# Forgetting attention followed by a tanh-shrink MLP: first-half rows first in the MLP, and q and k of batches 3 to 7 turned a slot sooner

## The chip, the core and the metric

The kernel runs on one core of a Trainium2 chip. A core has five engines with queues of their own: TensorE (PE in the profile; PEld is its weight loads), VectorE (DVE), ScalarE (ACT), GpSimd (POOL) and SyncE (SP). DMA transfers are issued by SP and POOL here. Each engine works through its queue strictly in the order in which it was written, and engines wait for one another and for transfers through semaphores. The metric is the device time of one execution in microseconds (us), lower is better; a kernel's time is the median of its runs.

## The reference

```python
scores = q @ k.T / sqrt(64)                      # 8 batches, 8 heads, 576 tokens, head size 64
cum    = cumsum(log(clip(f, 1e-4, 1)))           # per head, along the tokens
scores = where(causal, scores + cum[i] - cum[j], -1e9)
attn   = softmax(scores)                         # over j
x      = (attn @ v) as [8*576 tokens, 8*64]      # 4608 x 512
h      = x @ w_in                                # 512 -> 2048
out    = (h - tanh(h)) @ w_out                   # 2048 -> 512
```

## The kernel before

Attention runs over 32 pairs of heads, four pairs for each batch. The emission loop (lines 423 to 440) goes through 33 *slots* `p`. Slot `p` emits the seven score tiles of pair `p` (`scores`, numbered `ti` 0 to 6, each some matmuls, one exponential on ACT and a mask on POOL), after tile 2 the `values` products of the pair before, whose result DVE normalises into `xn` (lines 294 to 296), and after tile 3 the `turn` of that pair, two DMA transposes on SP that put `xn` into the ring `XR` with features on partitions (lines 310 and 312). `b` is a batch, and `p0 = 4(b-1)` is the first slot of the batch before it; the scores of batch `b` begin in slot `p0 + 4`.

The dictionary `LOADS` (lines 192 to 225) names further work by slot and tile: it is emitted right after the scores of that tile. For batches 3 to 7 this is

- `load_block`: one of five token blocks of q or k from HBM (POOL issues it, line 94);
- `turn_block`: a DMA transpose on SP (line 99) of one block into `TQ` or `TK`, single buffers with two heads on the 128 partitions;
- `place`: a DVE copy (line 102) of 64 partitions x 1152 elements from `TQ` or `TK` into `QT` or `KT`, the operands of the scores. It reads all tokens, so it needs all five transposes. A batch has four places for q and four for k.

Batches 0 to 2 come in another way (`trans`: TensorE transposes in the slot before, evicted by ACT for `QT`, line 242, and by DVE for `KT`, line 244).

The MLP works on nine *units* of 512 tokens. A unit is a list of 30 steps: 16 `mlp1` steps (four matmuls of 512 columns over the 512 features, then tanh on ACT, line 327, then DVE adds into `gq`, line 331), and 14 `mlp2` steps (eight matmuls of 256 columns each, line 352). `mlp2` is a Strassen-Winograd product: the 512 x 2048 input is cut into blocks A11, A12 (first 256 tokens; first and second half of the 2048 rows of `h`), A21, A22 (last 256 tokens), and seven products of the list `STEPS` (two steps each) replace eight. Their left sides S1 = A21 + A22, S2 = S1 - A11, S3 = A11 - A21 (written over A21) are DVE operations at line 337, in two groups of four row blocks each; S4 = A12 - S2 (over A12) is line 374. In step `s` of `mlp1` the half is `s % 2`: rows of both halves take turns, so every block is complete only after step 15. Results leave PSUM through ACT (`m1`, line 368) or DVE (line 358: outputs `ost` and running sums `u2`, `u3`), and go out by DMA from SP (line 364).

The steps are mixed into the slots: 15 in every two slots, so four slots hold the 30 steps of one unit, and the pattern repeats with each batch. One pool of four PSUM buffers (`ps_m`) serves `mlp1`, `mlp2` and the transposes of `trans`; `values` has one buffer. PE, DVE, POOL and SP run in exactly the order of emission; ACT's order is the scheduler's.

Of the kernel before, what the change touches and what calls it, by code (L numbers as in the profile page):

```python
# [8 lines left out]
FP32 = mybir.dt.float32  # L9
FP16 = mybir.dt.float16  # L10
AF = mybir.ActivationFunctionType
ALU = mybir.AluOpType
# [9 lines left out]
def kernel(  # L22
# [10 lines left out]
    nc = tc.nc  # L33
    P = 128
# [13 lines left out]
    HU = 256  # L48
    HE = DM // 2
    NCH = DM // P  # L50
    UW = 512
# [9 lines left out]
    acc = ctx.enter_context(tc.tile_pool(name="acc", bufs=1))  # L61
# [7 lines left out]
    W1 = wpl.tile([P, NK, HE], FP16)  # L69
    W2 = wpl.tile([P, NK, HE], FP16)  # L70
    W4 = wpl.tile([P, NK, HE], FP16)
    B11, B12 = wout[:, 0:NK, 0:HE], wout[:, 0:NK, HE:DM]
    B21, B22 = wout[:, NK:NFT, 0:HE], wout[:, NK:NFT, HE:DM]
# [6 lines left out]
    qb, kb = ([t[:, 0:NJ * DM].rearrange("p (n e) -> p n e", n=NJ) for t in raw] for raw in (qraw, kraw))  # L80
    vn = [qkp.tile([P, NJ, H, VW], FP16, tag=f"vn{i}", name=f"vn{i}") for i in range(2)]
    QT = [qkp.tile([D + 3, H, S], FP16, tag=f"QT{i}", name=f"QT{i}") for i in range(2)]
    KT = [qkp.tile([D + 3, H, PITCH], FP16, tag=f"KT{i}", name=f"KT{i}") for i in range(2)]
    TQ = qkp.tile([P, NPAIR, S], FP16, tag="TQ", name="TQ")
    TK = qkp.tile([P, NPAIR, S], FP16, tag="TK", name="TK")

    def load_qk(dst, src, b, h0, h1):
        nc.gpsimd.dma_start(
            out=dst[b % 2][:, h0:h1, :, :].rearrange("p h n d -> p h (n d)"),
            in_=src[b, h0:h1, :, :].rearrange("h (p n) d -> p h (n d)", n=NT6))  # L90

    def load_block(dst, src, b, n):
        pn = min(P, S - n * P)
        nc.gpsimd.dma_start(out=dst[b % 2][0:pn, n, :].rearrange("p (h d) -> p h d", h=H),  # L94
                            in_=src[b, :, n * P:n * P + pn, :].rearrange("h p d -> p h d"))

    def turn_block(dst, src, b, n):
        pn = min(P, S - n * P)
        nc.sync.dma_start_transpose(out=dst[:, :, n * P:n * P + pn], in_=src[b % 2][0:pn, n, :])

    def place(dst, src, b, a, c):
        nc.vector.tensor_copy(out=dst[b % 2][0:D, 2 * c + a:2 * c + 3 + a:2, 0:S], in_=src[a * D:(a + 1) * D, c:c + 2, :])  # L102
# [81 lines left out]
    def load_win(f0, f1):  # L184
        nc.gpsimd.dma_start(out=win[:, :, f0:f1],
                            in_=moe_w_in[:, f0:f1].rearrange("(c p) f -> p c f", p=P))

    def load_wout(t0, t1):
# [3 lines left out]
    LOADS = {(0, 1): [lambda: load_qk(qn, q, 1, 0, 2), lambda: load_qk(kn, k, 1, 0, 2)],  # L192
             (0, 4): [lambda: load_qk(qn, q, 1, 2, H)],
             (1, 0): [lambda: load_qk(kn, k, 1, 2, H)],
             (1, 2): [lambda: load_win(0, DFF // 2)],
             (1, 5): [lambda: load_v_rest(1), lambda: load_v_head(1, 0)],
             (2, 1): [lambda: load_v_head(1, 1), lambda: load_win(DFF // 2, DFF)],
             (4, 0): [lambda: load_wout(0, NFT // 2)],
             (4, 2): [lambda: load_wout(NFT // 2, NFT)]}
    for n in range(NJ - 1):  # L200
        LOADS.setdefault((3, n), []).append(lambda n=n: load_v_block(1, n, 2, H))
    for n in range(2):
        ks = slice(n * NK // 2, (n + 1) * NK // 2)
        for i, (o, x, y) in enumerate(((W1, B12, B11), (B12, B22, B12), (W2, B22, W1), (W4, B21, W2))):
            LOADS.setdefault((NPAIR + 1 + i // 2, (3, 5, 1, 4)[i] + n), []).append(lambda o=o, x=x, y=y, ks=ks: nc.vector.tensor_tensor(
                out=o[:, ks, :], in0=x[:, ks, :], in1=y[:, ks, :], op=ALU.subtract))
    LOADS.setdefault((NPAIR, 5), []).append(lambda: load_qk(qn, q, 2, 0, H))
    LOADS.setdefault((NPAIR, 6), []).append(lambda: load_qk(kn, k, 2, 0, H))
    for b in range(2, B):
        p0 = (b - 1) * NPAIR  # L210
        for n in range(NJ - 1):
            LOADS.setdefault((p0 + 1, n), []).append(lambda b=b, n=n: load_v_block(b, n, 0, H))
        LOADS.setdefault((p0 + 1, 4), []).append(lambda b=b: load_v_rest(b))
        LOADS.setdefault((p0, 0), []).append(lambda b=b: load_aug(b))
        if b < FAR:
            continue
        for n in range(NJ):
            LOADS.setdefault((p0 - 1, n), []).append(lambda b=b, n=n: load_block(qb, q, b, n))
            LOADS.setdefault((p0, n), []).append(lambda b=b, n=n: load_block(kb, k, b, n))
            LOADS.setdefault((p0, 4), []).append(lambda b=b, n=n: turn_block(TQ, qb, b, n))  # L220
            LOADS.setdefault((p0 + 1, 4), []).append(lambda b=b, n=n: turn_block(TK, kb, b, n))
        for n, (dst, src) in enumerate(((QT, TQ), (KT, TK))):
            for a in range(2):
                for c in (0, 2):
                    LOADS.setdefault((p0 + 3, 2 * n + a), []).append(lambda b=b, dst=dst, src=src, a=a, c=c: place(dst, src, b, a, c))

    E, XN, GQ, SQ, M2 = {}, {}, {}, {}, {}

# [83 lines left out]
        nc.sync.dma_start_transpose(out=XR[:, c, r0 + S - D:r0 + S], in_=xn[D:P, NJ - 1, :])  # L312

    def mlp1(u, s):
        pr, half = divmod(s, 2)
        ft = half * NK + pr
        hps = ps_m.tile([P, UW], FP32, tag="m", name="hps")
        t0 = u * UW % RING
        parts = [(0, t0, min(UW, RING - t0))]
        if t0 + UW > RING:  # L320
            parts.append((RING - t0, 0, t0 + UW - RING))
        for o, t, n in parts:
            for ci in range(NCH):
                nc.tensor.matmul(out=hps[:, o:o + n], lhsT=win[:, ci, ft * P:(ft + 1) * P],  # L324
                                 rhs=XR[:, ci, t:t + n], start=(ci == 0), stop=(ci == NCH - 1))
        th = tmp.tile([P, UW], FP32, tag="th", name="th")
        nc.scalar.activation(out=th, in_=hps, func=AF.Tanh, scale=-1.0)  # L327
        if s % 8 == 0:
            GQ[(u, s // 8)] = gtp.tile([P, 2, NK // 2, UW], FP16, tag="gq", name="gq")
        gq = GQ[(u, s // 8)]  # L330
        nc.vector.tensor_tensor(out=gq[:, half, pr % 4, :], in0=hps, in1=th, op=ALU.add)  # L331
        if s % 8 == 7:
            sq = SQ[(u, s // 8)] = gtp.tile([P, 2, NK // 2, HU], FP16, tag="sq", name="sq")
            a11, a21, a22 = gq[:, 0, :, 0:HU], gq[:, 0, :, HU:UW], gq[:, 1, :, HU:UW]
            for o, x, y, op in ((sq[:, 0], a21, a22, ALU.add), (sq[:, 1], sq[:, 0], a11, ALU.subtract),
                                (a21, a11, a21, ALU.subtract)):
                nc.vector.tensor_tensor(out=o, in0=x, in1=y, op=op)  # L337

    LHS = {"A11": lambda u, i: GQ[(u, i)][:, 0, :, 0:HU], "A12": lambda u, i: GQ[(u, i)][:, 1, :, 0:HU],
           "A22": lambda u, i: GQ[(u, i)][:, 1, :, HU:UW], "S3": lambda u, i: GQ[(u, i)][:, 0, :, HU:UW],  # L340
           "S1": lambda u, i: SQ[(u, i)][:, 0], "S2": lambda u, i: SQ[(u, i)][:, 1]}
    LHS["S4"] = LHS["A12"]
    STEPS = [("A11", B11), ("A12", B21), ("S2", W2), ("S3", B12), ("S1", W1), ("A22", W4), ("S4", B22)]

    def mlp2(u, s):
        n, m = divmod(s, 2)
        lhs, rhs = STEPS[n]
        if m == 0:
            M2["ps"] = ps_m.tile([P, 2, HE], FP32, tag="m", name="ops")
        ps = M2["ps"]  # L350
        for kt in range(NK):
            nc.tensor.matmul(out=ps[:, m, :], lhsT=LHS[lhs](u, kt // 4)[:, kt % 4, m * P:(m + 1) * P],  # L352
                             rhs=rhs[:, kt, :], start=(kt == 0), stop=(kt == NK - 1))
        if m == 0:
            return

        def plus(src, to):
            nc.vector.tensor_tensor(out=to, in0=ps, in1=src, op=ALU.add)  # L358
            return to

        def total(src, r, e):
            ost = plus(src, tmp.tile([P, 2, HE], FP32, tag="ost", name="ost", bufs=3))
            r0 = u * UW + r * HU
            nc.sync.dma_start(out=out[r0:r0 + HU, e * HE:(e + 1) * HE].rearrange("(m p) e -> p m e", p=P), in_=ost)

        if lhs == "A11":
            M2["m1"] = acc.tile([P, 2, HE], FP32, tag="m1", name="m1")
            nc.scalar.activation(out=M2["m1"], in_=ps, func=AF.Copy)
        elif lhs == "S2":
            M2["u2"] = plus(M2["m1"], acc.tile([P, 2, HE], FP32, tag="u2", name="u2"))  # L370
        elif lhs == "A12":
            total(M2["m1"], 0, 0)
            for i in range(2):
                nc.vector.tensor_tensor(out=LHS["S4"](u, i), in0=LHS["A12"](u, i), in1=LHS["S2"](u, i), op=ALU.subtract)
        elif lhs == "S3":
            M2["u3"] = plus(M2["u2"], acc.tile([P, 2, HE], FP32, tag="u3", name="u3"))
        elif lhs == "S1":
            total(M2["u3"], 1, 1)
            plus(M2["u2"], M2["u2"])
        elif lhs == "A22":  # L380
            total(M2["u3"], 1, 0)
        else:
            total(M2["u2"], 0, 1)
# [3 lines left out]
    def att_items(p):  # L387
# [29 lines left out]
        return items  # L417

    mlp = [(fn, u, s) for u in range(NU) for fn, n in ((mlp1, NFT), (mlp2, 2 * len(STEPS))) for s in range(n)]
    TAKE = (0, 0, 0, 0, 2, 7, 6, 6, 6)  # L420
    at = 0
    with tc.manual_schedule(engines={PE, mybir.EngineType.Pool, mybir.EngineType.SP, mybir.EngineType.DVE}):
        for p in range(len(pairs) + 1):
            b, c = divmod(p, NPAIR)
# [7 lines left out]
            given, n = 0, 0  # L432
# [38 lines left out]
```

## Time and profile before

| | |
|---|---|
| median of three runs | 369.44 us (369.12 to 370.68) |
| profiled execution | 373.72 us, span of its instructions 371.6 us |
| TensorE clock granted | 0.983 of full |
| busy of the span | PE 91%, DVE 76%, PEld 63%, ACT 58%, POOL 44% |
| DVE adds into `gq` (line 331) | 144 x 688 ns |
| DVE places (line 102) | 20 x 612 ns for `QT`, 20 x 583 ns for `KT` |
| DVE Strassen sums (line 337) | 54, 692 to 743 ns |

Busy PE time is modelled and counts matmuls that queue behind one another; idle time of an engine matters only where another engine waits for it. The profiled execution is one run with its own time, so sums made from its rows are read against 373.72 us and then carried to the median.

### The profile page before, as it was taken

The page shows a single profiled execution, that of the slowest core. Times are in us where ns is not written, and L with a number is a line of the kernel's source. Part 1 is how long each engine was busy: PE and PEld are TensorE (multiplying, and loading weights), DVE is VectorE, ACT ScalarE, POOL GpSimd, SP SyncE. Part 2 cuts the span into 40 slices and gives each one's busy share as a digit, 9 for nine tenths or more (in the row PEclk, how much of TensorE's full clock was granted, in tenths as well). Part 3 has the DMA queues.
Part 4 walks back from the last instruction along what each step waited for, and adds up shares of the span by engine and source line. Part 5 has one row for each costly group of instructions (what it writes and reads, how often), then busy time and mean ns, then how long its engine had stood idle before and what let it go on. Part 6 is the DMA issues. An engine that isn't in the chain of part 4 may idle for free.

```text
span 371.6 us, 8348 instructions
## 1 busy us (share of the span) xinstructions
PE 337.5 (91%) x3156; PEld 232.4 (63%) x3156; DVE 280.7 (76%) x477; ACT 215.6 (58%) x402; POOL 164.8 (44%) x340
## 2 busy tenths in 40 slices
PE   1798986999888999899989998999999999999995
PEld 0466543786447855685568886855685577477474
DVE  7575489876689569956995689668957885885873
ACT  6568886567854487448744774477547731531520
POOL 7977552586245744584457535752222220000000
PEclk9999899899989999999999999999999999999998
DMA  9999999699957997899499979996032013002002
GB/s 105 155 182 189 181 199 81 47 122 161 160 44 56 166 185 83 67 157 184 84 79 158 141 124 83 151 181 91 16 96 54 16 46 102 0 30 85 2 29 85
DMA packets 145323, 38.78 MB, mean 104 GB/s; under 512 B 128084, under 2 KB 144196, under 8 KB 145284
## 3 DMA queue, kind: packets, MB, share of 16 engines
q0 software_dynamic: 92416, 18.37, 66.2%
q1 hardware_dynamic: 52868, 19.90, 26.7%
q8 instruction: 24, 0.39, 0.5%
q14 instruction: 15, 0.12, 0.1%
HBM read 36.85 MB, written 9.44 MB: 125 GB/s over the span
## 4 chain that ended last, share of the span: by engine, by line
PE 55%; DVE 25%; ACT 9%; issue 6%; DMA 3%; POOL 1%; POOLq 0%; DVEq 0%; SPq 0%; ACTq 0%
PE ops L352 26%; PE hps L324 13%; PE ps L266 9%; DVE gq L331 8%; ACT e L272 4%; PE av L290 4%; ACT th L327 4%; DVE QT L102 3%; DVE sq L337 3%; DVE xn L296 3%; DVE KT L244 2%; PE t L235 2%; DMA XR<-xn 2%; DVE KT L102 1%; DVE gq L337 1%
## 5 line engine op out<-in xcount | busy, mean ns | idle before, releaser
L324 PE MATMUL hps<-XR,win 128*128 128x512 f16 (+1 forms) x640 | 144.0, 362 | 5.1 <-DVE gq L331 3.9
L272 ACT ACTIVATE e<-ps 128x512 f16<-128x512 f32 x192 | 111.7, 601 | 43.7 <-PE ps L266 41.9
L327 ACT ACTIVATE th<-hps 128x512 f32<-128x512 f32 x144 | 87.0, 606 | 66.1 <-PE hps L324 54.4
L331 DVE TENSOR_TENSOR gq<-hps,th 128x512 f16<-128x512 f32 x144 | 97.7, 688 | 34.2 <-ACT th L327 32.7
L280 POOL TENSOR_SCALAR_AFFINE_SELECT e<-e 128x128 f16<-128x128 f16 (+1 forms) x192 | 67.0, 352 | 100.8 <-ACT e L272 98.9
L324 PEld LDWEIGHTS <-win 128*128 128x128 f16 x640 | 58.6, 98 | 55.9 <-issue 10.2
L266 PE MATMUL ps<-QT,KT 67*128 67x64 f16 (+4 forms) x384 | 80.0, 295 | 11.5 <-DMA KT<-clo 4.6
L352 PEld LDWEIGHTS <-gq 128*128 128x128 f16 x720 | 67.6, 98 | 21.8 <-DVE gq L331 10.2
L352 PE MATMUL ops<-wout,gq 128*128 128x256 f16 x576 | 74.6, 275 | 7.2 <-DVE gq L331 7.0
L266 PEld LDWEIGHTS <-KT 67*128 67x128 f16 x384 | 37.8, 103 | 37.3 <-issue 14.3
L358 DVE TENSOR_TENSOR ost<-ops,u 128x512 f32<-128x512 f32 x27 | 18.7, 691 | 28.1 <-PE ops L352 28.0
L290 PEld LDWEIGHTS <-e 128*128 128x128 f16 x896 | 34.3, 100 | 4.7 <-POOL e L280 1.0
L352 PE MATMUL ops<-W,sq 128*128 128x256 f16 x288 | 36.4, 272 | 0.0
L290 PE MATMUL av<-vn,e 128*128 128x65 f16 x896 | 35.3, 197 | 0.9 <-POOL e L280 0.9
L352 PEld LDWEIGHTS <-sq 128*128 128x128 f16 x288 | 27.1, 97 | 4.8
L113 POOL DMA_DIRECT2D vn<-in_v_dram x32 | 27.9, 874 | 2.3 <-issue 2.3
L296 DVE TENSOR_TENSOR xn<-av,rs 128x640 f16<-128x640 f32 x32 | 26.4, 824 | 1.1
L94 POOL DMA_DIRECT2D qn<-in_q_dram x25 | 21.2, 846 | 2.6 <-issue 2.6
L94 POOL DMA_DIRECT2D kn<-in_k_dram x25 | 21.1, 845 | 1.8 <-issue 1.7
L280 POOL TENSOR_SCALAR_AFFINE_SELECT el<-el 128x128 f16<-128x128 f16 x32 | 9.7, 303 | 26.8 <-ACT el L272 26.5
L244 DVE COPY KT<-t 64x576 f16<-64x576 f16 x24 | 19.1, 797 | 0.3
L352 PE MATMUL ops<-W,gq 128*128 128x256 f16 x144 | 18.2, 272 | 0.0
(58 smaller groups left out, 230.6 us busy)
## 6 DMA issues: line engine op xcount, KB each, us to landing
out_dram<-ost SPq DMA_DIRECT2D x36, 256.0 KB
vn<-in_v_dram POOLq DMA_DIRECT2D x24, 128.0 KB, 5.6
qn<-in_q_dram POOLq DMA_DIRECT2D x20, 128.0 KB, 3.8
kn<-in_k_dram POOLq DMA_DIRECT2D x20, 128.0 KB, 4.6
win<-in_moe_w_in_dram POOLq DMA_DIRECT2D x2, 1024.0 KB, 11.8
wout<-in_moe_w_out_dram POOLq DMA_DIRECT2D x2, 1024.0 KB, 11.0
XR<-xn SPq DMA_TRANSPOSE x56
vn<-in_v_dram POOLq DMA_DIRECT2D x12, 64.0 KB, 5.0
```

The source lines that it names most:

```text
L94: nc.gpsimd.dma_start(out=dst[b % 2][0:pn, n, :].rearrange("p (h d) -> p h d", h=H), in_=src[b, :, n * P:n * P + pn, :].rearrange("h p d - ...
L113: nc.gpsimd.dma_start(out=vn[b % 2][:, n, h0:h1, 0:D], in_=v[b, h0:h1, n * P:(n + 1) * P, :].rearrange("h p d -> p h d"))
L244: nc.vector.tensor_copy(out=to, in_=of)
L266: nc.tensor.matmul(out=ps[:, col:col + n], lhsT=KT[b % 2][:, h, j * P:(j + 1) * P], rhs=QT[b % 2][:, h, i0:i0 + n])
L272: nc.scalar.activation(out=e[:, lo:hi], in_=ps[:, lo:hi], func=AF.Exp, scale=qscale)
L280: nc.gpsimd.affine_select(out=view, in_=view, compare_op=ALU.is_ge, fill=0.0, base=0, pattern=pat, channel_multiplier=-1)
L290: nc.tensor.matmul(out=av[:, a, ib, :], lhsT=E.pop((b, c, a, j, ib)), rhs=vn[b % 2][:, j, 2 * c + a, 0:D + 1], start=(j == 0), stop=(j == ib))
L296: nc.vector.tensor_tensor(out=xn.rearrange("p i (a d) -> p a i d", a=2), in0=av[:, :, :, 0:D], in1=rs.to_broadcast([P, 2, NJ, D]), op=ALU. ...
L324: nc.tensor.matmul(out=hps[:, o:o + n], lhsT=win[:, ci, ft * P:(ft + 1) * P], rhs=XR[:, ci, t:t + n], start=(ci == 0), stop=(ci == NCH - 1))
L327: nc.scalar.activation(out=th, in_=hps, func=AF.Tanh, scale=-1.0)
L331: nc.vector.tensor_tensor(out=gq[:, half, pr % 4, :], in0=hps, in1=th, op=ALU.add)
L352: nc.tensor.matmul(out=ps[:, m, :], lhsT=LHS[lhs](u, kt // 4)[:, kt % 4, m * P:(m + 1) * P], rhs=rhs[:, kt, :], start=(kt == 0), stop=(kt ...
```

## The change

Three things are edited.

1. `mlp1` takes four steps of the first half, then four of the second, and again. A11 and A21 are complete after step 11 rather than 15. S3 is made as soon as a group's first half is there (`s % 8 == 3`); at `s % 8 == 7` S2 is made from A22 and S3, and S1 from S2 and A11.
2. `STEPS` puts S3 second: A11, S3, A12, S2, S1, A22, S4. The result of the S3 product is now copied out of PSUM by ACT (a second copy of 128 x 512 elements in each unit), and `u3` is the DVE sum of two SBUF tiles.
3. For batches 3 to 7 the loads and transposes of q and k are emitted one slot sooner. The eight places, which all stood in slot `p0 + 3`, are spread: four for `QT` in slot `p0` after tiles 0, 2, 4 and 6, two for `KT` in slot `p0 + 2` and two in slot `p0 + 3`, after tiles 1 and 5.

```diff
-            LOADS.setdefault((p0 - 1, n), []).append(lambda b=b, n=n: load_block(qb, q, b, n))
-            LOADS.setdefault((p0, n), []).append(lambda b=b, n=n: load_block(kb, k, b, n))
-            LOADS.setdefault((p0, 4), []).append(lambda b=b, n=n: turn_block(TQ, qb, b, n))
-            LOADS.setdefault((p0 + 1, 4), []).append(lambda b=b, n=n: turn_block(TK, kb, b, n))
-        for n, (dst, src) in enumerate(((QT, TQ), (KT, TK))):
-            for a in range(2):
-                for c in (0, 2):
-                    LOADS.setdefault((p0 + 3, 2 * n + a), []).append(lambda b=b, dst=dst, src=src, a=a, c=c: place(dst, src, b, a, c))
+            LOADS.setdefault((p0 - 2, n), []).append(lambda b=b, n=n: load_block(qb, q, b, n))
+            LOADS.setdefault((p0 - 1, n), []).append(lambda b=b, n=n: load_block(kb, k, b, n))
+            LOADS.setdefault((p0 - 1, 4), []).append(lambda b=b, n=n: turn_block(TQ, qb, b, n))
+            LOADS.setdefault((p0, 4), []).append(lambda b=b, n=n: turn_block(TK, kb, b, n))
+        spots = ((p0, 0), (p0, 2), (p0, 4), (p0, 6), (p0 + 2, 1), (p0 + 2, 5), (p0 + 3, 1), (p0 + 3, 5))
+        parts = [(dst, src, a, c) for dst, src in ((QT, TQ), (KT, TK)) for a in range(2) for c in (0, 2)]
+        for spot, (dst, src, a, c) in zip(spots, parts):
+            LOADS.setdefault(spot, []).append(lambda b=b, dst=dst, src=src, a=a, c=c: place(dst, src, b, a, c))
...
-        pr, half = divmod(s, 2)
+        half, pr = s % 8 // 4, s // 8 * 4 + s % 4
...
+        a11, a21, a22 = gq[:, 0, :, 0:HU], gq[:, 0, :, HU:UW], gq[:, 1, :, HU:UW]
+        if s % 8 == 3:
+            nc.vector.tensor_tensor(out=a21, in0=a11, in1=a21, op=ALU.subtract)
         if s % 8 == 7:
             sq = SQ[(u, s // 8)] = gtp.tile([P, 2, NK // 2, HU], FP16, tag="sq", name="sq")
-            a11, a21, a22 = gq[:, 0, :, 0:HU], gq[:, 0, :, HU:UW], gq[:, 1, :, HU:UW]
-            for o, x, y, op in ((sq[:, 0], a21, a22, ALU.add), (sq[:, 1], sq[:, 0], a11, ALU.subtract),
-                                (a21, a11, a21, ALU.subtract)):
-                nc.vector.tensor_tensor(out=o, in0=x, in1=y, op=op)
+            nc.vector.tensor_tensor(out=sq[:, 1], in0=a22, in1=a21, op=ALU.subtract)
+            nc.vector.tensor_tensor(out=sq[:, 0], in0=sq[:, 1], in1=a11, op=ALU.add)
...
-    STEPS = [("A11", B11), ("A12", B21), ("S2", W2), ("S3", B12), ("S1", W1), ("A22", W4), ("S4", B22)]
+    STEPS = [("A11", B11), ("S3", B12), ("A12", B21), ("S2", W2), ("S1", W1), ("A22", W4), ("S4", B22)]
...
-        if lhs == "A11":
-            M2["m1"] = acc.tile([P, 2, HE], FP32, tag="m1", name="m1")
-            nc.scalar.activation(out=M2["m1"], in_=ps, func=AF.Copy)
-        elif lhs == "S2":
-            M2["u2"] = plus(M2["m1"], acc.tile([P, 2, HE], FP32, tag="u2", name="u2"))
+        if lhs in ("A11", "S3"):
+            M2[lhs] = acc.tile([P, 2, HE], FP32, tag=lhs, name="m" + lhs)
+            nc.scalar.activation(out=M2[lhs], in_=ps, func=AF.Copy)
         elif lhs == "A12":
-            total(M2["m1"], 0, 0)
+            total(M2["A11"], 0, 0)
             for i in range(2):
                 nc.vector.tensor_tensor(out=LHS["S4"](u, i), in0=LHS["A12"](u, i), in1=LHS["S2"](u, i), op=ALU.subtract)
-        elif lhs == "S3":
-            M2["u3"] = plus(M2["u2"], acc.tile([P, 2, HE], FP32, tag="u3", name="u3"))
+        elif lhs == "S2":
+            M2["u2"] = plus(M2["A11"], acc.tile([P, 2, HE], FP32, tag="u2", name="u2"))
+            M2["u3"] = acc.tile([P, 2, HE], FP32, tag="u3", name="u3")
+            nc.vector.tensor_tensor(out=M2["u3"], in0=M2["u2"], in1=M2["S3"], op=ALU.add)
```

## The prediction, made before the changed kernel was run

> **What bounds the kernel now.** I read the page's chain first, then the waits of PE, then a table of DVE and PE by period, then DVE's and SP's timelines around a slot boundary.
>
> ```profile
> PE 55%; DVE 25%; ACT 9%; issue 6%; DMA 3%; POOL 1%; POOLq 0%; DVEq 0%; SPq 0%; ACTq 0%
> PE ops L352 <- DVE gq L331: 7.0, 10, 1.0
> ```
>
> PE sets the end for about half of the span, DVE for a quarter. The wait is the start of `mlp2`: A11's last block needs the `gq` of step 14, A12's that of step 15.
>
> ```profile
> core 0: us, PE busy (x) PEld busy (x) DVE busy (x) ACT busy (x) POOL busy (x), PEclk, DMA share, GB/s
> 114.62:152.38 37.76, 35.89 (x344) 24.05 (x344) 29.87 (x53) 23.02 (x45) 21.94 (x43) 1.00 1.35 125
> 152.38:190.15 37.77, 35.90 (x344) 24.06 (x344) 29.88 (x53) 23.05 (x46) 22.03 (x43) 1.00 1.18 123
> 190.15:228.02 37.87, 36.05 (x408) 30.32 (x408) 29.91 (x53) 23.15 (x46) 22.00 (x43) 1.00 1.26 124
> 228.02:264.77 36.75, 35.69 (x344) 24.06 (x344) 28.86 (x53) 22.75 (x46) 18.46 (x39) 1.00 1.15 114
> ```
>
> The cuts are the ends of `xn` in the slots `p0 + 3` of batches 3 to 7 (slots 11, 15, 19, 23, 27). Each row is one period: four slots, one unit. PE idles 1.9 us of 37.8, DVE 7.2 us by the gaps between its instructions over 0.08 us; so DVE is occupied 30.5 us (29.9 busy and small gaps). The next two lists show where DVE is full and how long SP needs for a turn.
>
> ```profile
> 189.33 0.82 DVE L296 TENSOR_TENSOR xn<-av,rs 128x640 f16<-128x640 f32 x1
> 190.07 0.68 DVE L331 TENSOR_TENSOR gq<-hps,th 128x512 f16<-128x512 f32 x1
> 190.79 0.69 DVE L337 TENSOR_TENSOR sq<-gq 128x1024 f16<-128x1024 f16 x1
> 191.51 0.69 DVE L337 TENSOR_TENSOR sq<-sq,gq 128x1024 f16<-128x1024 f16 x1
> 192.12 0.79 DVE L337 TENSOR_TENSOR gq<-gq 128x1024 f16<-128x1024 f16 x1
> 192.94 1.03 DVE L102 COPY KT<-TK 64x1152 f16<-64x1152 f16 x2
> ```
>
> ```profile
> 190.22 1.20 SPq L310 DMA_TRANSPOSE XR<-xn  x1
> 191.47 1.23 SPq L312 DMA_TRANSPOSE XR<-xn  x1
> ...
> 201.22 7.67 SPq L99 DMA_TRANSPOSE TQ<-qn  x5
> 208.98 1.75 SPq L364 DMA_DIRECT2D out_dram<-ost  x2
> 210.83 1.29 SPq L310 DMA_TRANSPOSE XR<-xn  x1
> ```
>
> DVE runs without a gap from `xn` (slot 19) into slot 20. SP issues the two transposes of `XR` right after `xn`, each taking 1.2 us of SP, and five transposes of q take it 7.7 us.
>
> **The change, part by part.**
>
> *The waits at the start of `mlp2`.* After the change A11 and S3 read only rows finished at step 11, so four steps of some 1.1 us each stand before the first reader of step 15. This removes at most the 7.0 us of the wait row: 0.8 us in slot 7 (the first A11 step takes 1.71 us of the chain in place of 0.88) and 1.6 in each of the periods that begin in slots 11, 15, 19 and 23. It is worth something only where DVE does not set the pace instead.
>
> *The Strassen sums.* Three DVE operations per group before and after, of the same shape (692 to 743 ns): nothing. But a group's block at `s % 8 == 7` is two operations long, not three. In the two last units, which have no attention beside them, `mlp1` waited 0.61 us each time for the block: 1.2 us gained (0 to 1.2). Slot 10 gains another 0.8 where `KT` copies stand behind the block.
>
> *ACT's second copy*: nine of 0.60 us (the row of line 368). ACT is busy 23 of 37.8 us and the copy falls into `mlp2`, where ACT waits for PE (13.2 us before the first copy): nothing; without that cover 5.4 us. *`u3` from SBUF*: 9 DVE sums as before, bounded by 0.68 us (from PSUM) and 0.74 (the f16 sum in SBUF): nothing.
>
> *Loads and POOL.* The same 50 issues of 0.85 us, one slot sooner; a slot that held k loads (`p0`) is now empty of loads. POOL is 44% busy: nothing. Its first load in slot 6 waits for nothing late, as the data it overwrites was turned one slot before.
>
> *The q turn, moved on SP.* SP's order in slot `p0 - 1` (the last slot of a period) becomes: `XR` of that slot, which waits for `xn`, then five `TQ` transposes, then the three rows of line 160 to 162, then `ost`. The first place for q stands in slot `p0` right behind the last `KT` place, in front of A12's `ost`, the S4 sums and `xn`. So DVE comes to a place whose transposes start only after the `xn` that it has just made. Time from the end of `xn` to the fifth landing: 0.07 + 2.6 us of `XR` (from 210.83 to the first `TK` at 213.49 in the row's continuation), then the turn. From first issue to last landing, by the semaphore updates in the trace, five turns of k under light traffic took 7.6, 8.0, 8.5, 8.1 and 8.1 us, five turns of q beside the v loads 11.1, 10.7, 10.4, 12.4 and 10.5. After the change no v loads stand beside the q turn (they come two slots later), only the tail of k: I take 8.0, nearest to k's turns, and keep 12.4 as the other end. Landing is thus 10.7 us after `xn`. DVE's work until then is `gq`, two sums and a place: 0.7 + 1.4 + 0.6 = 2.7 us. **DVE stands still for 8.0 us** (7.6 to 12.4), once per batch.
>
> *What that does in a period.* Before, DVE's 7.2 idle us were spread over it, each beside PE work. Now 8.0 lie in one piece, and everything behind queues. Shortest period for DVE: 30.5 + 8.0 = 38.5, if it never waits elsewhere. It will: `xn` of slot `p0` is ready some 4.5 us after the landing, its `XR` transposes land 2.4 to 5.3 us later (both ends seen in slots `p0`), and the next unit's first `mlp1` step reads them; PE there needs 17.3 us to the next `values`, and `xn` 1.2: 4.5 + 4 + 0.5 + 17.3 + 1.2 + 10.7 = 38.2, so PE and DVE hand over just in time. The k turn, now beside the v loads, may cost up to 1 us. I take 39.0 (38.3 to 41). Against 37.8, 37.8, 37.9 and 36.75: +1.2, +1.2, +1.1 and +2.25, in all **+5.8 us** (+3 to +14). The 1.6 us of waits and the 2.4 us of q places taken out of the full stretch lie inside these periods: they shorten PE's path, which no longer sets it.
>
> *Batch 3 is worse*, since slots 8 to 10 still hold `KT` copies for batch 2 on DVE.
>
> ```profile
> 72.46 1.21 SPq L310 DMA_TRANSPOSE XR<-xn  x1
> 73.71 1.23 SPq L312 DMA_TRANSPOSE XR<-xn  x1
> 80.48 1.61 DVE L244 COPY KT<-t 64x576 f16<-64x576 f16 x2
> 82.45 0.68 PE L266 MATMUL ps<-QT,KT 67*128 67x320 f16 x3
> ```
>
> The turn starts at 75.0 and lands at 83.0; DVE gets to the place at 77.7. Behind it stand place, `u2`, `u3`, place, `xn`: 0.6 + 0.7 + 0.7 + 0.6 + 1.2, then the two copies of line 244 (1.6), done at 88.4 in place of 82.1. The scores of slot 9 read them, and PE, in order, would reach these at 82.9: **+5.5 us** (+3 to +8). Of this the next stretch gives back the 0.8 of slot 10 and 1.4 in slots 10 and 11, where DVE has fewer places before `xn`: -2.2.
>
> *After the last turn* (slot 27) PE has done A11 and S3 but not A12 by `xn`: +0.5.
>
> **Sum**: -0.8 + 5.5 - 2.2 + 5.8 + 0.5 - 1.2 = +7.6 us. The profiled execution, 373.72 us (span 371.6 and 2.1 around it), stands 4.3 above the median; it would go to 381.3, and the median from 369.44 to 377.0.
>
> A page's price for the turn: the Trainium skill ("DMA: Bandwidth & Descriptors", Anatomy of one DMA) fits a transfer to about 2.0 us plus its bytes over 436 GB/s, and "Advanced Engine Details and Errata" (X-Bar Transpose) calls transposes as fast as other DMAs; an estimate by them for 590 KB is 3.4 us, and DVE would stand 3.4 us, not 8.0. One block under no load (131 KB, 2.3 by that rule) took 2.3 to 2.5 us here, so the trace agrees for one; for five in a row it does not, as SP issues them 1.3 us apart.
>
> **Rivals.**
>
> *A, the sum above*: 372.5 to 383, most likely 377.0. Chance 0.55.
>
> *B, the wait is covered (other side).* Place: the first q place of slot `p0`. PE has seven products and four PSUM buffers; if the fifth transpose lands within 37.8 - 30.5 + 2.7 = 10.0 us of `xn`, DVE's stop is no longer than the idle time it had, PE sets the period, and its idle time goes: 6.6 us over the four periods (150.15 - 143.53), 0.8 and 1.2 beside. 369.4 - 8.6 = 360.8 (357 to 367.5, the high end if batch 3 still pays). For it: the margin is 0.7 us per period. Against: no row shows a turn under 7.6, and then DVE may never wait anywhere else. Chance 0.13.
>
> *B2, the five transposes overlap* and land together, one block's 2.4 us after the first issue: DVE would stand 2.7 + 2.4 - 2.7 = 2.4 us, well inside its idle time, and the time is B's, 360.8. All ten turns speak against it: 0.02. The Trainium skill's rule above speaks for this case.
>
> *C, even periods*: the stop just fits, and only batch 3 and the last period pay: 369.4 - 0.8 + 5.5 - 2.2 + 0.5 - 1.2 = 371.2 (369 to 372.5). Chance 0.14.
>
> *D, the turn stays as slow as q's were* (11.0 in place of 8.0): +3.0 in five places on top of A, 392 (383 to 396). For it: all five q turns. Against: their neighbours, the v loads, move away. Chance 0.16.
>
> **How the numbers follow.** The time is A's. Low end 369, where C begins (B's 0.15 left out); high end 390, which leaves out a third of D: about 0.2 outside. A's own range is 372.5 to 383. A measurement of this kernel tells about 0.5% (1.85 us) from no change. Faster: B and B2 and a little of C, 0.16; within 0.5%: half of C, 0.07; slower: 0.77.
>
> **What would show it.** Right: in DVE's list a gap of about 8 us before the first `QT` place of each slot `p0`, with line 102 now waiting for the DMA `TQ`; the 7.0 us row of line 352 gone; periods near 39 between the `xn` ends; in slot 9 PE waiting some 5 us for line 244; `XR` ending PE's wait at the first `mlp1` step. Wrong: a gap under 7 us, or periods of 36 with DVE gaps spread as before.

## The result, and the profile after

The changed kernel takes **386.85 us** (median of four runs, 386.75 to 388.63) against 369.93 (369.12 to 370.68) for the kernel before in the same comparison: **1.047 times the time before (95% interval 1.043 to 1.051), 16.9 us slower**. The forecast was slower by 7.6 us, to 377.0. The direction and the mechanism were right and the time lies inside the range, but the loss is more than twice the forecast, and it lies outside the likeliest case's own range of 372.5 to 383. The profiled execution of the change took 386.75 us, with a span of 385.0. Medians and ranges are of all runs, while ratios leave out a run that is more than 1.5% above the fastest of its kernel.

The first two lines are the busy time of each engine and the chain that ended last, the third is the group of the q places, all from the page of the changed kernel.

```profile
PE 338.7 (88%) x3156; PEld 232.3 (60%) x3156; DVE 276.0 (72%) x477; ACT 220.3 (57%) x411; POOL 171.1 (44%) x340
PE 30%; DVE 6%; DMA 6%; ACT 4%; SPq 4%; issue 3%; POOL 1%; POOLq 0%; DVEq 0%; ACTq 0%
L102 DVE COPY QT<-TQ 64x1152 f16<-64x1152 f16 x20 | 9.6, 499 | 40.7 <-DMA TQ<-qn 40.5
```

PE is busy 338.7 us where it was busy 337.5: over the whole span it is the gaps that have grown. The chain of the second line reaches back only to 172.7 us, so its shares sum to 54% of the span, where those of before sum to 99%. In this part transfers and SP's issuing have 10 of the 54, where they had 3 of 99, and DVE has 6. The 40.7 us behind the bar of the third line are time in which DVE did nothing at all, and 40.5 of them ended with a transpose of q. The waits of the changed kernel, with total, number and longest:

```profile
DVE QT L102 <- DMA TQ<-qn: 40.5, 5, 9.2
PE ps L266 <- DVE KT L244: 9.9, 4, 5.7
PE hps L324 <- DMA XR<-xn: 9.0, 3, 4.0
PE ops L353 <- DVE gq L373: 2.2, 3, 1.8
```

The 7.0 us wait at the start of `mlp2` (for line 331) has gone as the prediction said. In its place stand five stops of DVE of 8.1 us each on average, and three kinds of wait behind them (of the first kind the kernel before had 3.1 us). This is one such stop in DVE's timeline (start, duration, and in brackets the idle time before the instruction), at the boundary of slots 19 and 20:

```profile
193.31 0.82 DVE L296 TENSOR_TENSOR xn<-av,rs 128x640 f16<-128x640 f32 x1
194.05 0.68 DVE L331 TENSOR_TENSOR gq<-hps,th 128x512 f16<-128x512 f32 x1
194.76 0.69 DVE L337 TENSOR_TENSOR sq<-gq 128x1024 f16<-128x1024 f16 x1
195.49 0.69 DVE L338 TENSOR_TENSOR sq<-sq,gq 128x1024 f16<-128x1024 f16 x1
196.21 0.46 DVE L102 COPY KT<-TK 64x1152 f16<-64x1152 f16 x1
205.28 0.58 DVE L102 COPY QT<-TQ 64x1152 f16<-64x1152 f16 x1 [8.61 <-DMA TQ<-qn]
...
208.60 0.82 DVE L296 TENSOR_TENSOR xn<-av,rs 128x640 f16<-128x640 f32 x1
```

And this is SP, which issues the transfers, in the same stretch:

```profile
194.20 1.20 SPq L310 DMA_TRANSPOSE XR<-xn  x1
195.45 1.22 SPq L312 DMA_TRANSPOSE XR<-xn  x1
196.76 7.16 SPq L99 DMA_TRANSPOSE TQ<-qn  x5
...
209.49 1.23 SPq L310 DMA_TRANSPOSE XR<-xn  x1
```

SP must first issue the two transposes of `XR`, which need the `xn` that ended at 194.13; then five of q. DVE is at the place after 2.5 us of work and stands until 205.28, 11.2 us after that `xn`. The next `xn` queues behind the place and ends at 209.4, its transposes start at 209.49, and PE needs them:

```profile
210.38 0.93 PE L324 MATMUL hps<-XR,win 128*128 128x256 f16 x7
215.30 0.37 PE L324 MATMUL hps<-XR,win 128*128 128x256 f16 x1 [3.99 <-DMA XR<-xn]
...
215.58 3.60 PE L324 MATMUL hps<-XR,win 128*128 128x256 f16 x16
...
219.41 1.89 PE L324 MATMUL hps<-XR,win 128*128 128x256 f16 x8
...
221.35 1.04 PE L324 MATMUL hps<-XR,win 128*128 128x256 f16 x8
```

Here is what the forecast lacked. After PE's stop of 3.99 us, sixteen matmuls of 256 columns take 3.60 us, and from 221 on eight take 1.04 or less: PE runs at half its speed for a while. The windows of the changed kernel between the same `xn` ends that cut the periods before (columns: window, length, busy time of each engine, granted TensorE clock, DMA share, GB/s) show it:

```profile
core 0: us, PE busy (x) PEld busy (x) DVE busy (x) ACT busy (x) POOL busy (x), PEclk, DMA share, GB/s
114.91:155.14 40.23, 36.91 (x337) 24.29 (x336) 28.87 (x53) 23.23 (x46) 22.76 (x42) 0.96 1.22 113
155.14:194.13 38.99, 35.92 (x346) 24.12 (x345) 28.62 (x52) 23.64 (x46) 23.54 (x43) 1.00 1.48 119
194.13:237.79 43.66, 39.02 (x410) 31.68 (x409) 29.00 (x53) 23.78 (x46) 23.87 (x43) 0.92 1.16 108
237.79:278.62 40.83, 37.58 (x346) 24.40 (x343) 28.39 (x53) 23.74 (x46) 16.77 (x36) 0.96 0.72 94
```

The period with a clock of 1.00 takes 38.99 us: the forecast's 39.0. The other three have clocks of 0.96, 0.92 and 0.96, and are 1.2, 4.7 and 1.8 us longer. In the trace's record of the granted clock, half speed comes in stretches of 3.41 and 6.83 us: from 129.0 (3.41), 214.3 (6.83) and 258.7 (3.41). Before, the four periods had none. PE's busy time in the four sums to 149.4 us where it was 143.5, for the same matmuls, and its idle time to 14.3 where it was 6.6. So of the 13.6 us by which the four periods grew, 5.9 are matmuls that took longer and 7.7 are waiting.

Between the same cuts the whole difference of the two profiled executions is

| stretch | before | after | difference | forecast |
|---|---|---|---|---|
| start to `xn` of slot 3 | 33.8 | 30.7 | -3.1 | 0 |
| slots 3 to 7 | 38.7 | 37.1 | -1.6 | -0.8 |
| slots 7 to 11 (batch 3) | 42.2 | 47.1 | +4.9 | +3.3 |
| slots 11 to 27 (four periods) | 150.2 | 163.7 | +13.6 | +5.8 |
| slots 27 to 31 | 34.9 | 35.7 | +0.8 | +0.5 |
| slot 31 to the end | 72.0 | 70.8 | -1.2 | -1.2 |

The instructions up to slot 3 are the same in both kernels, so the first row is not the change (the last section shows where it comes from). The other rows sum to +16.5 us, near the +16.9 of the medians.

### The profile page after: what moved, and what is told of

The parts are those of the page before. It is cut to its first block, busy times and chain, and to the rows that moved or that the text cites. A ratio compares the mean times of both kernels' runs of the same rounds, so it can differ in the third digit from the quotient of the medians.

```text
span 385.0 us, 8355 instructions
## 1 busy us (share of the span) xinstructions
PE 338.7 (88%) x3156; PEld 232.3 (60%) x3156; DVE 276.0 (72%) x477; ACT 220.3 (57%) x411; POOL 171.1 (44%) x340
## 4 chain that ended last, share of the span: by engine, by line
PE 30%; DVE 6%; DMA 6%; ACT 4%; SPq 4%; issue 3%; POOL 1%; POOLq 0%; DVEq 0%; ACTq 0%
PE hps L324 14%; PE ops L353 13%; SPq L99 3%; DMA XR<-xn 3%; ACT e L272 2%; PE ps L266 2%; DVE gq L331 2%; ACT th L327 2%; PE av L290 2%; DMA TQ<-qn 1%; DVE xn L296 1%; DMA kn<-in_k_dram 1%; DMA TK<-kn 1%; DVE gq L373 1%; DVE sq L337 1%
## 5 line engine op out<-in xcount | busy, mean ns | idle before, releaser
L324 PE MATMUL hps<-XR,win 128*128 128x512 f16 (+1 forms) x640 | 146.9, 367 | 13.1 <-DMA XR<-xn 9.0
L280 POOL TENSOR_SCALAR_AFFINE_SELECT e<-e 128x128 f16<-128x128 f16 (+1 forms) x192 | 73.1, 386 | 94.5 <-ACT e L272 92.8
L331 DVE TENSOR_TENSOR gq<-hps,th 128x512 f16<-128x512 f32 x144 | 96.4, 686 | 24.2 <-ACT th L327 22.4
L266 PE MATMUL ps<-QT,KT 67*128 67x64 f16 (+4 forms) x384 | 78.3, 287 | 20.7 <-DVE KT L244 9.9
L324 PEld LDWEIGHTS <-win 128*128 128x128 f16 x640 | 59.5, 99 | 55.7 <-issue 8.4
L353 PEld LDWEIGHTS <-gq 128*128 128x128 f16 x720 | 69.0, 100 | 17.7 <-DVE gq L373 4.0
L102 DVE COPY QT<-TQ 64x1152 f16<-64x1152 f16 x20 | 9.6, 499 | 40.7 <-DMA TQ<-qn 40.5
L290 PEld LDWEIGHTS <-e 128*128 128x128 f16 x896 | 33.4, 99 | 5.3 <-POOL e L280 0.9
L353 PE MATMUL ops<-W,sq 128*128 128x256 f16 x288 | 35.4, 272 | 0.0
L359 DVE TENSOR_TENSOR ost<-ops,u 128x512 f32<-128x512 f32 x27 | 18.3, 690 | 10.8 <-PE ops L353 9.7
```

Source lines behind the costliest of these rows:

```text
L266: nc.tensor.matmul(out=ps[:, col:col + n], lhsT=KT[b % 2][:, h, j * P:(j + 1) * P], rhs=QT[b % 2][:, h, i0:i0 + n])
L280: nc.gpsimd.affine_select(out=view, in_=view, compare_op=ALU.is_ge, fill=0.0, base=0, pattern=pat, channel_multiplier=-1)
L290: nc.tensor.matmul(out=av[:, a, ib, :], lhsT=E.pop((b, c, a, j, ib)), rhs=vn[b % 2][:, j, 2 * c + a, 0:D + 1], start=(j == 0), stop=(j == ib))
```

## Experiments

The theory after the result: DVE's stop at the first q place delays `xn`, so `XR`, so PE; PE's stops then cost a second time, in TensorE's clock. Rivals: the MLP half of the change slows the kernel by itself; the move of loads and transposes to earlier slots does, without the places; the half clock follows the stops but is no cause of time; the clock has nothing to do with PE's idle time. Each job's runs stand beside runs of the kernel before on the same chip: medians 373.25 us for the first four experiments, 369.01 for the next three, 370.89 for the last four.

### The MLP half alone, and the q and k half alone

The first keeps the loads, transposes and places of q and k where they were and takes the new step order, `STEPS` and Strassen sums. The second is the reverse.

```diff
 # MLP half alone
-            LOADS.setdefault((p0 - 2, n), []).append(lambda b=b, n=n: load_block(qb, q, b, n))
+            LOADS.setdefault((p0 - 1, n), []).append(lambda b=b, n=n: load_block(qb, q, b, n))
...
+                    LOADS.setdefault((p0 + 3, 2 * n + a), []).append(lambda b=b, dst=dst, src=src, a=a, c=c: place(dst, src, b, a, c))
 # q and k half alone
-        half, pr = s % 8 // 4, s // 8 * 4 + s % 4
+        pr, half = divmod(s, 2)
...
-    STEPS = [("A11", B11), ("S3", B12), ("A12", B21), ("S2", W2), ("S1", W1), ("A22", W4), ("S4", B22)]
+    STEPS = [("A11", B11), ("A12", B21), ("S2", W2), ("S3", B12), ("S1", W1), ("A22", W4), ("S4", B22)]
```

> The MLP part alone (first-half rows first, S3 product second), q and k loaded, turned and placed as before. Theory (all of the loss is the q places that wait in slot p0): no wait of line 102 on a DMA, the 7.0 us of mlp2 on gq gone, 361 to 368 us against 369.9. Rival (the reordered MLP itself costs, through ACT's second copy or the later PSUM releases): 372 us or more.

> The q and k part alone, MLP as before. Theory: five waits of line 102 on the transposes of some 8 us each, 384 to 394 us (the MLP part is worth 0 to 6 us, so a little above the full change's 386.9). Rival (the reordered MLP costs): 378 us or less.

Measured: MLP half alone 361.21 us (359.8 to 362.52), ratio 0.968 (0.960 to 0.977); q and k half alone 388.83 (382.8 to 391.66), ratio 1.032 (1.020 to 1.044). The first has no wait of line 102 for a transfer, and its four periods are 35.90, 35.67, 35.78 and 34.44 us. The second has the stop:

```profile
DVE QT L102 <- DMA TQ<-qn: 32.1, 5, 7.8
```

with periods of 38.96, 38.20, 43.68 and 41.13 us. So the MLP half gains and the q and k half loses. They do not add up: on top of the stop the MLP half is worth nothing that shows (386.85 and 388.83, in different comparisons, with ranges that overlap), because PE no longer sets the period's length. Its gain of 8.5 to 12 us is there only when PE does.

### The same places one slot later

Everything of the change stays but the four q places, which move from slot `p0` to slot `p0 + 1`. The transposes are as early as in the change.

```diff
-        spots = ((p0, 0), (p0, 2), (p0, 4), (p0, 6), (p0 + 2, 1), ...
+        spots = ((p0 + 1, 0), (p0 + 1, 2), (p0 + 1, 4), (p0 + 1, 6), (p0 + 2, 1), ...
```

> The full change, with the four q places one slot later (p0 + 1 in place of p0), so that loads and transposes keep their earlier slots and only the reading DVE copies come later. Theory: no wait on the transposes is left and the time falls below the kernel before: 358 to 367 us. Rival (the earlier loads and transposes cost by themselves, through SP's queue or DMA contention): 375 us or more.

Measured: 369.42 us (363.31, 367.89, 370.94 and 372.43), ratio 0.982 (0.969 to 0.994). The stop for `TQ` is gone, and with it at least 17 us of the loss; early loads and transposes alone do not slow the kernel. Of the four runs only the lowest lies inside what was expected, and the two lower ones, on which the ratio rests, are 2 and 7 us above the MLP half's median. The profile is of the slowest of the four and has a new wait, at the k places:

```profile
DVE KT L102 <- DMA TK<-kn: 3.8, 3, 2.1
```

Periods were 39.64, 37.0, 36.5 and 37.4 us. The k turn now stands beside the loads of v, as the prediction feared of it; that this and DVE's fuller slot `p0 + 1` are why the kernel stays above the MLP half is argued from this row of its slowest run, not shown.

### The transposes of q ahead of XR

The places stay as early as in the change. What makes DVE wait is moved: q's five transposes are emitted after tile 2 of slot `p0 - 1` in place of tile 4, so that they stand ahead of the two transposes of `XR` on SP and need not wait for `xn`.

```diff
-            LOADS.setdefault((p0 - 1, 4), []).append(lambda b=b, n=n: turn_block(TQ, qb, b, n))
+            LOADS.setdefault((p0 - 1, 2), []).append(lambda b=b, n=n: turn_block(TQ, qb, b, n))
```

> The full change, with the five q transposes emitted after score tile 2 of slot p0 - 1 in place of tile 4, so that on SP they stand ahead of the two XR transposes of that slot and do not wait for its xn. The q places stay in slot p0. Theory (the stop comes from the order on SP: turn behind XR behind xn): the DVE gap of 8 to 9 us before the first q place shrinks to 0 to 3 us, XR of that slot comes some 6 us later, and the time is 358 to 369 us. Rival (five transposes one slot sooner are too slow or in the way wherever they stand on SP): 376 us or more.

> The full change with the q transposes ahead of XR on SP. If the earlier q and k part is worth something once DVE is not stopped for long (2.4 us of q places out of the full stretch of each period), 2 to 8 us below the MLP part alone. If PE sets both, within 1.5 us of it.

> The MLP part alone, on the same chip as the full change with the q transposes first: 359 to 364 us.

Measured: 361.35 us (359.12 to 363.46), ratio 0.976 (0.969 to 0.984). Again, in the last job: 361.15 (358.15 to 363.92), ratio **0.974 (0.968 to 0.980)**, beside the MLP half alone with 362.37 (357.66 to 362.58), ratio 0.976 (0.970 to 0.983). Two tiles in the emission order turn a loss of 4.6% into a gain of 2.6%. The waits, two windows, and SP at the start of a turn, all of the second run of this kernel:

```profile
DVE QT L102 <- DMA TQ<-qn: 11.0, 4, 4.4
```

```profile
109.93:145.70 35.77, 35.31 (x345) 24.13 (x344) 29.33 (x53) 23.74 (x46) 23.16 (x43) 1.00 1.20 124
145.70:181.59 35.89, 35.41 (x346) 24.21 (x345) 28.92 (x52) 23.75 (x46) 23.31 (x43) 1.00 1.28 131
```

```profile
176.50 6.61 SPq L99 DMA_TRANSPOSE TQ<-qn  x5
183.22 1.21 SPq L310 DMA_TRANSPOSE XR<-xn  x1
```

The turn starts at 176.50, five us before the `xn` that ends at 181.59, where in the change it started 2.6 us after one. DVE still stops, for up to 4.4 us where 0 to 3 were expected, and it costs nothing: PE is busy 35.3 to 35.4 of 35.8 us, at full clock, and `XR`, now behind five transposes on SP and issued 1.6 us after its `xn` (some 6 later was expected), ends no wait of PE. And the two kernels of the last job are the same within their spread: once its stop costs nothing, the q and k half is worth nothing beside the MLP half.

### Batch 3's q places alone one slot later

```diff
-        spots = ((p0, 0), (p0, 2), (p0, 4), (p0, 6), (p0 + 2, 1), ...
+        pq = p0 + (b == FAR)
+        spots = ((pq, 0), (pq, 2), (pq, 4), (pq, 6), (p0 + 2, 1), ...
```

> The full change, with batch 3's four q places alone one slot later (slot 9 in place of 8); batches 4 to 7 as in the change. Theory (batch 3 pays 4.9 us from slot 7 to slot 11, because KT copies for batch 2 stand behind its stop, and the half clock after that): the PE wait of 5.7 us in slot 9 goes, 380 to 383 us against 386.9. Rival (batch 3's stop is covered, the loss is in the later periods): 386 to 388 us.

Measured: 382.31 us (381.63 to 383.96), ratio 1.034 (1.027 to 1.040). The stretch from slot 7 to slot 11 went from 47.1 to 40.88 us, and one of the five stops is gone:

```profile
DVE QT L102 <- DMA TQ<-qn: 34.6, 4, 9.3
```

The medians lie only 4.5 to 5.3 us apart, as expected. So batch 3's stop is a part of the loss and not most of it: 13.3 us remain against before, with four stops left and periods of 40.04, 38.37, 42.04 and 41.09 us, together 11.4 above those of before.

### Is it the clock? PE kept busy through the stops

PE's stops stay, but it runs matmuls whose results are overwritten, on operands that are there: 24 ahead of the scores of slot 9, and some ahead of the first `mlp1` step of units 3, 4 and 5. They add work to the kernel, which no output needs.

```diff
+FILL = {3: 9, 4: 14, 5: 10}
...
+        if (b, c, ti) == (2, 1, 0):
+            for i in range(24):
+                nc.tensor.matmul(out=ps, lhsT=win[:, 0, 0:P], rhs=win[:, i % NCH, 512:512 + UW])
...
+        if s == 0:
+            for i in range(FILL.get(u, 0)):
+                nc.tensor.matmul(out=hps, lhsT=win[:, 0, 0:P], rhs=win[:, i % NCH, 512:512 + UW])
```

> The full change with extra matmuls on PE (results overwritten) only where PE stood still in its profile: 24 of 512 columns (5.2 us) before the scores of slot 9, and 9, 14 and 10 of them (1.9, 3.0, 2.2 us) before the first mlp1 step of units 3, 4 and 5. They take PE no longer than it waited. Theory (a good part of the 16.9 us is TensorE's clock, granted at half for 3.4 to 6.8 us after each such stop): 379 to 383.5 us, and fewer half-clock stretches. Rival (the clock is only a companion, DVE paces those stretches anyway): 386 to 389 us.

Measured: 384.59 us (382.43 to 388.41), ratio 1.031 (1.022 to 1.039): between the two ranges expected, 379 to 383.5 and 386 to 389, so it decides nothing by itself. The stretches at half clock from 81, 214 and 258 were gone. But the period from slot 11 had a new stop, at the first step of unit 2, where nothing was filled, and with it 6.83 us of half clock:

```profile
134.80 0.59 PE L331 MATMUL hps<-XR,win 128*128 128x512 f16 x1 [3.02 <-DMA XR<-xn]
```

That period took 42.92 us, the other three 39.7 to 40.0. So the filling was extended to unit 2 (`FILL = {2: 13, 3: 9, 4: 14, 5: 10}`), and timed twice, the second time beside the change itself.

> The kernel with the filling matmuls, 13 more of them (2.8 us) before the first mlp1 step of unit 2, where PE stood still for 3.0 us in its profile and a half-clock stretch of 6.8 us followed. Theory (a period without half clock is 39 to 40 us, one with 3.4 us of it 40 to 41, one with 6.8 us 43 to 44): no half-clock stretch between 110 and 280 us, that period falls from 42.9 to 39 to 40 us, 378.5 to 382.5 us in all. Rival (the longer periods have another cause): that period stays above 42 us.

> The full change again, on the same chip as the next three, so that they can be compared with it: 385 to 389 us. Both views of the clock expect this.

> The full change with all five long PE stops filled by matmuls whose results are overwritten. If half-clock stretches cost what the periods suggest (1.5 us for 3.4 us of half clock, 4 us for 6.8), 3 to 6 us less than the full change on the same chip. If the clock is only a companion: within 1.5 us of it.

Measured: first 383.49 us (381.55 to 385.11), ratio 1.036 (1.028 to 1.045), 1 us above what was expected. No half clock was left in the four periods, and the first took 41.0 us, where 39 to 40 were expected and the rival said above 42. In the last job: the change 387.58 (384.61 to 389.25), ratio 1.046 (1.040 to 1.052); the filled kernel 382.72 (380.24 to 384.52), ratio 1.033 (1.027 to 1.039). **With 70 matmuls more, it is 4.9 us faster**, and its slowest run is below the change's fastest. The four periods of the change in this job, and then of the filled kernel:

```profile
114.91:154.76 39.85, 35.30 (x337) 23.34 (x336) 28.66 (x53) 23.23 (x46) 22.84 (x42) 1.00 1.11 114
154.76:195.39 40.63, 36.92 (x346) 24.57 (x345) 28.90 (x53) 23.74 (x46) 23.62 (x43) 0.96 1.12 115
195.39:238.28 42.89, 38.61 (x410) 31.64 (x409) 28.88 (x53) 23.79 (x46) 23.66 (x43) 0.92 1.14 109
238.28:279.88 41.60, 37.58 (x344) 24.41 (x343) 28.57 (x53) 23.74 (x46) 17.16 (x36) 0.96 0.75 92
```

```profile
114.69:155.46 40.77, 38.91 (x361) 25.61 (x360) 29.04 (x53) 23.75 (x46) 23.70 (x44) 1.00 1.16 113
155.46:195.24 39.78, 38.01 (x355) 25.01 (x354) 28.90 (x52) 23.75 (x46) 24.32 (x43) 1.00 1.13 118
195.24:234.37 39.13, 38.71 (x424) 31.81 (x423) 28.83 (x52) 23.78 (x46) 23.21 (x43) 1.00 1.18 120
234.37:273.70 39.33, 38.06 (x355) 24.94 (x354) 28.46 (x52) 23.68 (x46) 17.07 (x36) 1.00 0.81 97
```

Every clock of the second list is 1.00, and the four periods sum to 159.0 in place of 165.0 us. DVE's stops are still there (39.2 us in these periods and batch 3), so it was not by shortening them that the filling gained. That the clock follows PE's idle time, and that it costs time, is shown. What is not: how much more than 4.9 us it costs in all, since at slot 9 and at unit 4 no wait is left behind the filling, which may delay real work there. From the forecast's 4 x 39.0 = 156.0, the filled kernel's periods are 3.0 us away, and these are open.

The Trainium skill ("TensorE: Matmul & The Clock Gate", Part 1: The HAM clock gate) tells of a free-running window of 3.41 us after which an idle TensorE goes to half rate, and back after a busy one. The trace agrees on the lengths, 3.41 and twice that, and on the two rates: sixteen matmuls of 256 columns in 3.41 us of the chain at 215.77, then eight in 0.88. It differs on what suffices: the last section has half clock after windows in which PE was busy for almost half of the time.

## Why the prediction was right or wrong

- **DVE stands still for 8.0 us once per batch** (7.6 to 12.4): right. Five stops of 5.7, 9.2, 8.3, 8.6 and 8.8 us. The landing was forecast 10.7 us after `xn`; the stops ended 11.3, 11.8, 10.8, 11.2 and 11.3 us after it. The choice of the k turns' 8.0 us as the price, not the 11 of the q turns, was right: DVE went on 7.7 to 9.2 us after the first of the five transposes was issued. The smaller stop is batch 3's, where DVE came later to the place.
- **The wait at the start of `mlp2` goes, and is worth something only where DVE does not set the pace**: right. The row is gone; the MLP half alone gained 8.5 us (last job) to 12 (first), where rival B put this gain at 8.6; in the change's four periods none of it is seen.
- **Batch 3, +5.5 and -2.2**: mechanism right, and PE waited 5.68 us for line 244 in slot 9, as named ("some 5 us"). The stretch measured +4.9, not +3.3. The filled kernel's stretch, which like the one before has a single 3.41 us at half clock, took 45.46, so +3.3; the change had 6.83 us at half clock after that stop. The same term is missing here.
- **The periods, +5.8**: this is the step that failed; measured +13.6, at the very end of its range of +3 to +14. Its mechanism held to the end: `XR` ended PE's wait at the first `mlp1` step, three times, by 2.38, 3.99 and 2.61 us, and the one period without half clock took 38.99 us for the predicted 39.0. What the sum lacked was a term for TensorE's clock. All rows of before stood at 1.00, and the forecast let PE's time per matmul be the same after stops that the kernel before had not had. The three other periods were 1.2, 4.7 and 1.8 us over 39.0, 7.7 of the 7.8 us by which the four were missed. The four hold 13.65 us at half speed, which can take at most 6.8 us of PE's work away; PE's busy time grew by 5.9, which the sum had at nothing, and filling the stops gave 4.9 back. Waiting grew by 7.7 where the sum had 5.8; that is the other 1.9. That 38.99 met 39.0 so closely is in part luck: in the other three profiles with these stops and no filling, periods without half clock took 38.2 to 39.9 us.
- **A way to see it beforehand** was in the profile of before: its own trace has stretches of 3.41 us at half clock from 65.8 and 103.3, right behind two of its PE stops, of 2.55 and 2.49 us (PE's timeline of the kernel before), both outside the four periods:

```profile
64.86 0.39 PE L266 MATMUL ps<-QT,KT 67*128 67x512 f16 x1 [2.55 <-DVE KT L244]
...
103.24 1.84 PE L324 MATMUL hps<-XR,win 128*128 128x512 f16 x4 [2.49 <-DVE gq L331]
```

  A forecast that makes PE wait 2 to 5 us five times more could have taken an estimate of 1.7 us for each, half of 3.41.
- **Slot 7, -0.8; tail, -1.2; after slot 27, +0.5**: measured -1.6, -1.2 and +0.8.
- **The k turn beside v's loads, up to 1 us**: in the change itself no place waits for `TK`. Where the k places came under pressure (q places one slot later), it was 3.8 us in three places.
- **The rivals.** B, the wait covered, gave 360.8 us with the point at 10.0 us from `xn` to landing; the change had 10.8 to 11.8 and fell on the other side. But its price was right: with the transposes ahead of `XR`, the stop ended before it mattered, and the time is 361.2. B2, overlapping transposes, is out: SP issued q's five over 6.5 to 8.0 us in the change. The 3.4 us that the prediction estimates by the Trainium skill ("DMA: Bandwidth & Descriptors", Anatomy of one DMA) did not come either (7.7 to 9.2 us); the rule there is fitted to transfers that GpSimd issues, and SP issues these. C is out, since the periods were not even. D came to a time near the measured one (392, from 383), but by a mechanism that did not occur: the turn was not slow (7.7 to 9.2 us, not 11).

## What to carry to other kernels

A wait that stops an engine in the middle of its queue is priced by everything queued behind it, and costs nothing until some of that comes late: here four stops of up to 4.4 us of DVE were free, and five of 8 us on average cost 17 us and swallowed the whole gain of another edit. When a forecast makes TensorE wait a few microseconds where it had not, add the time at half clock behind each wait, and look in the trace of before for a stop of that length and the clock after it. Before moving a reader earlier, follow its transfer through the issuing queue: whether it stands before or behind something that waits for this very engine decided the sign here.

## What the runs showed of the hardware

- Half clock came in stretches of 3.41 or 6.83 us, and short stops sufficed. PE's stop of 1.79 us before 128.4 was followed by 3.41 us at half clock, that of 2.61 us before 257.5 too, those of 3.99 and 5.68 us by 6.83. The length of a stop alone does not decide: that of 2.38 us before 174.1 was followed by none. What does is in the traces. In each of the thirteen profiles all steps of the granted clock lie whole multiples of 3.413 us after the first step, so PE's activity seems to be judged in fixed windows of that length. Four such windows of the change (columns as above):

```profile
125.57:128.98 3.41, 1.62 (x14) 0.99 (x11) 2.31 (x5) 1.51 (x3) 2.62 (x4) 1.00 0.16 24
169.94:173.35 3.41, 1.71 (x34) 1.20 (x33) 3.17 (x7) 0.00 (x0) 2.49 (x4) 1.00 1.40 118
210.90:214.31 3.41, 0.41 (x4) 0.21 (x3) 3.33 (x7) 0.00 (x0) 1.01 (x2) 1.00 2.89 116
255.27:258.69 3.42, 1.19 (x8) 0.59 (x8) 3.29 (x9) 0.77 (x2) 0.35 (x1) 1.00 1.69 169
```

  The first, third and fourth were followed by half clock, the second, with PE busy for 1.71 us, was not: the stop of 2.38 us lies across its end. Over all profiles from 45 us on there are 1192 windows at full clock. All 32 with PE busy for under 43% of the window were followed by half clock, 6 of the 8 between 43% and 48%, and none of the 1152 above. (Earlier, at 38 us, four profiles have it after 58 to 59%, which stays open.) In the other profile of the change the windows lie otherwise against the work: PE was busy for 1.82 us of the one that ended at 129.20, and no half clock followed; for 0.92 us of the one that ended at 173.59, and it did. The same kernel's periods so differ by up to 1.6 us between these two profiles.
- SP was held 1.2 to 1.3 us by each DMA transpose, so that five in a row took 6.5 to 8.0 us of its queue, and the transposes behind them started no earlier.
- The first 30 us differ by 3 us between executions of the same instructions. In the profiled execution of before `xn` of slot 3 ended at 33.8 us, in that of the change at 30.7. The difference goes with the clock: its record begins, at full, at 31.6 us in the one and at 19.8 in the other, and the same two score matmuls took 0.63 us in the one and 0.38 in the other (before, then after):

```profile
24.00 0.63 PE L266 MATMUL ps<-QT,KT 67*128 67x320 f16 x2
```

```profile
22.36 0.38 PE L266 MATMUL ps<-QT,KT 67*128 67x320 f16 x2
```

  All thirteen profiles fit: where the record begins at 19.7 to 20.0 us, `xn` ended at 30.7 to 30.8 (four profiles); where it begins at 24.6 to 25.8, at 32.0 to 32.8 (five); where it begins at 31.2 to 31.6, at 33.1 to 33.8 (four). What decides when the full clock comes stayed open; it is of the size of the distance between the profiled execution of before (373.72) and its median.
